# Emitting a convolution and an MLP as one interleaved instruction stream, with work moved between VectorE, ScalarE and GpSimd

## The chip, the cores and the metric

The kernel runs on one core of one Trainium2 chip. The metric is the device time of one execution in microseconds (us), as a median of several executions. The "span" of a profile runs from the first to the last instruction and is some 2 us shorter than the time of the same execution. A run carries a state, fast or slow. All comparisons here use fast runs.

A ratio below is the mean time of one kernel's fast runs over the mean time of the other's fast runs of the same rounds. It is therefore not quite the ratio of the medians that stand beside it. The square brackets after a ratio are its 95% interval.

Names of engines in the profile: PE is TensorE (matmul), PEld its weight load, DVE is VectorE, ACT is ScalarE, POOL is GpSimd, SP is SyncE, which issues DMAs here. A name with a q at its end, such as SPq, is that engine's sequencer.

## The reference, cut to what matters

The input is one sequence of 2048 tokens with 640 channels. Two branches read it, and a gate of one value per token mixes them.

```python
x = A_q                                             # [1, 2048, 640], bf16
g = sigmoid((x * gate_w).sum(-1, keepdims=True))    # gate

# branch A: long convolution
k_shift = sum over t < 4 of shifted(k, 3-t) * shift_k[:, t]   # short filter, "k shift"
kv = k_shift * v
y  = irfft(rfft(kv, 4096) * rfft(ssm_k, 4096))[:2048] + kv * ssm_D
a  = q * y

# branch B: token mixer, then MLP
h  = gelu(layernorm(x) @ w1)                        # 640 -> 640
x1 = x + token_shifted(h) @ w2
b  = x1 + gelu(layernorm(x1) @ w3) @ w4             # 640 -> 1536 -> 640
return g * a + (1 - g) * b
```

## The kernel before

All data stay on the chip. A *slab* is 128 tokens (one per partition), and there are 16 of them. The Fourier transforms are matmuls. The channels are split into two halves `dh` and the frequencies into two halves `h`, so there are four rounds. Each round has an *h pass* (transform of the filter) and an *x pass* (transform of `kv`, product with the filter, first half of the inverse). After the two rounds of a channel half comes `inv`. Between the two stages of a transform, data must change partitions, and that is a DMA from SBUF to SBUF, the *exchange*: `GR` to `gx` in a pass, `VR` to `vx` in the inverse.

```python
def exchange(dst, stage, lo):
    nc.sync.dma_start(out=dst, in_=stage.rearrange("(a r) t d -> a r t d", a=8)[:, lo])

def step1(src, dh, h, isH):                 # first stage: 16 matmuls, 8 ScalarE copies to GR
    ...
def x_pass(dh, h):
    step1(KV, dh, h, False)
    for kp in range(T1 // 2):               # 8 pairs
        ps = pst()
        gx = ring.tile([P, 2, DH], BF16, name="gx", bufs=3)
        for j in range(2):
            exchange(gx[:, j, :], GR, 2 * kp + j)
            nc.tensor.matmul(ps[:, j, 0:DH], lhsT=M3[:, 0, :], rhs=gx[:, j, :], ...)
        xs = ring.tile([P, 2, DH], BF16, name="xs")
        nc.scalar.copy(out=xs[:], in_=ps[:, :, 0:DH])
        pq = ring.tile([P, 2, 2, DH], BF16, name="pq", tag="pv", bufs=3)
        nc.vector.tensor_tensor(out=pq[:], in0=xs[:]..., in1=HH[:, 2 * kp:2 * kp + 2], op=ALU.mult)
        pv = pst()
        for j in range(2):                  # needs pq of this very pair
            nc.tensor.matmul(pv[:, j, 0:DH], lhsT=M3[:, 1, :], rhs=pq[:, j, 0, :], ...)
            nc.tensor.matmul(pv[:, j, 0:DH], lhsT=M3[:, 2, :], rhs=pq[:, j, 1, :], ...)
        nc.scalar.copy(out=VR[:, h, 2 * kp:2 * kp + 2, :], in_=pv[:, :, 0:DH])

def inv(dh):
    for tp in range(T1 // 2):
        ...
            for h in range(2):
                exchange(vx[:, j, h, :], VR[:, h], t1)       # 64 transfers of 80 KB in all
                nc.tensor.matmul(ps[:, j, 0:DH], lhsT=I1[:, h, t1, :], rhs=vx[:, j, h, :], ...)
        nc.vector.tensor_tensor(out=g, in0=ps[:, :, 0:DH], in1=g, op=ALU.mult)
# ... cut: layer norms, W1, W2, gate, k shift ...
w1_chunk(0) ... gate(); mix_shift(); h_pass(0, 0)
for s in range(T1): w2_slab(s)
i1_transposes(); kshift(0) ... kshift(3)
x_pass(0, 0); h_pass(0, 1); w3_chunk(0); x_pass(0, 1); w4_chunk(0)
h_pass(1, 0); gq_half(0); inv(0); w3_chunk(1); x_pass(1, 0); h_pass(1, 1)
w4_chunk(1); w3_chunk(2); x_pass(1, 1); gq_half(1); inv(1)
# ... cut: adds and stores around w4_chunk(2), w3_chunk(3), w4_chunk(3)
```

The traces show the stages on every engine in the order of these calls, with small overlaps only: in the last inverse some w4 matmuls (L461, written later) run between inverse matmuls (L428) from 472.05 us on.

Of the kernel before, what the change touches and what calls it, by code (L numbers as in the profile page):

```python
# [24 lines left out]
def kernel(  # L25
# [55 lines left out]
    R9 = big.tile([P, DT * Fh], BF16, name="R9")  # L81
# [3 lines left out]
    VR = R3.rearrange("p (h t d) -> p h t d", h=2, t=T1)  # L85
    KRG = R3[:, 0:2 * 7 * D].rearrange("p (b t d) -> p b t d", b=2, t=7)
# [6 lines left out]
    ACC = R4[:, 5 * D:7 * D].rearrange("p (t d) -> p t d", t=2)  # L93
    KTMP = R4[:, 7 * D:11 * D].rearrange("p (b t d) -> p b t d", b=2, t=2)
    CJB = GR[:, 0:8, :].rearrange("p k d -> p (k d)")
    MIX = I1[:, 0]
    GEN = HT.rearrange("p t d -> p (t d)")
    NANG = R11[:, 0:8192].bitcast(I32)
    W1 = R9[:, 0:DT * D].rearrange("p (k e) -> p k e", k=DT)
    W2 = R9[:, DT * D:2 * DT * D].rearrange("p (k e) -> p k e", k=DT)  # L100
    W1M = R9[:, 2 * DT * D:2 * DT * D + D].rearrange("p (k e) -> p k e", k=DT)
    W3 = R9.rearrange("p (k f) -> p k f", k=DT)
# [4 lines left out]
    for c in range(4):  # L107
        nc.sync.dma_start(out=QX[:, 4 * c:4 * c + 4, :], in_=q3[:, 4 * c:4 * c + 4, :])
# [10 lines left out]
    def load_k(c):  # L119
        kr = KRG[:, c % 2]  # L120
        if c == 0:
            nc.gpsimd.memset(kr[0:1, 0:3, :], 0.0)
            nc.sync.dma_start(out=kr[1:113, 0:3, :], in_=k3[0:112, 13:16, :])
            nc.sync.dma_start(out=kr[113:128, 0:3, :], in_=k3[112:127, 13:16, :])
            nc.sync.dma_start(out=kr[:, 3:7, :], in_=k3[:, 0:4, :])
        else:
            nc.sync.dma_start(out=kr[:], in_=k3[:, 4 * c - 3:4 * c + 4, :])
        nc.sync.dma_start(out=KV[:, 4 * c:4 * c + 4, :], in_=v3[:, 4 * c:4 * c + 4, :])

    load_k(0)  # L130
    load_k(1)
    for gi in range(4):
        nc.sync.dma_start(out=W2[:, gi, :], in_=B_w2[gi * CG:gi * CG + P, :])
        nc.sync.dma_start(out=W2[32 * gi:32 * gi + 32, 4, :], in_=B_w2[gi * CG + P:(gi + 1) * CG, :])

# [19 lines left out]
    BPI = cons.tile([P, 1], F32, name="BPI")  # L155
    nc.vector.memset(BPI[:], -PI)
    s16 = f32(iot(T1, [[1, T1]], 0, T1), T1)
    wcol = f32(iot(256, [[128, 2], [0, 2], [2, 64]], 1), 256)
    ocol = f32(iot(256, [[0, 2], [-2048, 2], [0, 64]], 6144), 256)
    for g in range(4):  # L160
        n1 = NANG[:, g * 1024:(g + 1) * 1024]
        for j in range(4):
            t1 = 4 * g + j
            nc.vector.scalar_tensor_tensor(out=n1[:, j * 256:(j + 1) * 256], in0=wcol, scalar=s16[:, t1:t1 + 1],
                                           in1=ocol, op0=ALU.mult, op1=ALU.add)
        nc.vector.tensor_scalar(out=n1, in0=n1, scalar1=8191, scalar2=None, op0=ALU.bitwise_and)
        nc.scalar.activation(out=F1[:, 4 * g:4 * g + 4, :, :].rearrange("p a b c -> p (a b c)"), in_=n1,
                             func=ACT.Sin, scale=PI / 4096, bias=BPI[:])

    M3 = cons.tile([P, 3, P], BF16, name="M3")  # L170
    prow = iot(1, [[1, 1]], 0, 1)
    tr = gtile(3, I32)
    for i, bits in enumerate((15, 48, 64)):
        nc.vector.tensor_scalar(out=tr[:, i:i + 1], in0=prow, scalar1=bits, scalar2=None, op0=ALU.bitwise_and)
    trf = f32(tr, 3)
    N3 = 3 * P
    ck1f = f32(iot(N3, [[0, 24], [1, 16]]), N3)
    cof = gtile(N3, I32)
    for m, (stp, b0) in enumerate(((12, 12), (4, 12), (4, 8))):
        nc.gpsimd.iota(cof[:, m * P:(m + 1) * P], pattern=[[stp, 2], [0, 64]], base=b0, channel_multiplier=0)  # L180
    coff = f32(cof, N3)
    crm = gtile(N3, F32)
    for m, val in enumerate((4.0 / 64, 8.0 / 64, 0.0)):
        nc.gpsimd.memset(crm[:, m * P:(m + 1) * P], val)
    cklf = f32(iot(P, [[0, 2], [16, 4], [0, 16]]), P)
    an = gtile(N3, F32)
    nc.vector.scalar_tensor_tensor(out=an, in0=ck1f, scalar=trf[:, 0:1], in1=coff, op0=ALU.mult, op1=ALU.add)
    ani = gtile(N3, I32)
    nc.vector.scalar_tensor_tensor(out=ani, in0=crm, scalar=trf[:, 2:3], in1=an, op0=ALU.mult, op1=ALU.add)
    nc.vector.tensor_scalar(out=ani, in0=ani, scalar1=15, scalar2=None, op0=ALU.bitwise_and)  # L190
    sn = gtile(N3, F32)
    nc.scalar.activation(out=sn, in_=ani, func=ACT.Sin, scale=PI / 8, bias=BPI[:])
    mask = gtile(P, F32)
    nc.vector.tensor_scalar(out=mask, in0=cklf, scalar1=trf[:, 1:2], scalar2=None, op0=ALU.is_equal)
    for m in range(3):
        nc.vector.tensor_tensor(out=M3[:, m, :], in0=sn[:, m * P:(m + 1) * P], in1=mask, op=ALU.mult)
# [4 lines left out]
    ONE1 = cons.tile([1, P], BF16, name="ONE1")  # L201
    nc.gpsimd.memset(ONE1[:], 0.0)
    nc.gpsimd.memset(ONE1[:, 0:64], 1.0)
    NHALF = cons.tile([P, T1], F32, name="NHALF")
    nc.gpsimd.memset(NHALF[:], -0.5)
# [8 lines left out]
    def stats_group(slabs):  # L214
        n = len(slabs)
        st = ring.tile([P, n, 2, 6], F32, name="bst")
        mv = ring.tile([P, n, 2], F32, name="mv")
        for i, s in enumerate(slabs):
            for j in range(2):
                nc.vector.bn_stats(out=st[:, i, j, :], in_=QX[:, s, j * DH:(j + 1) * DH])  # L220
            nc.vector.bn_aggr(out=mv[:, i, :], in_=st[:, i, :, :])
        ve = ring.tile([P, n], F32, name="ve")
        nc.gpsimd.tensor_scalar(out=ve[:], in0=mv[:, :, 1], scalar1=1e-5, scalar2=None, op0=ALU.add)
        rs = ring.tile([P, n], F32, name="rs")
        nc.gpsimd.tensor_tensor(out=rs[:], in0=ve[:], in1=NHALF[:, 0:n], op=ALU.pow)
        nb = ring.tile([P, n], F32, name="nb")
        nc.vector.scalar_tensor_tensor(out=nb[:], in0=mv[:, :, 0], scalar=-1.0, in1=rs[:], op0=ALU.mult, op1=ALU.mult)
        return rs, nb

    def norm_transpose(slabs, rs, nb, dst, eng, after=None):  # L230
        for i0 in range(0, len(slabs), 2):
            pt = pst16()
            for j in range(2):
                s = slabs[i0 + j]
                xn = ring.tile([P, D], BF16, name="xn", tag="xy", bufs=3)
                nc.vector.tensor_scalar(out=xn[:], in0=QX[:, s, :], scalar1=rs[:, i0 + j:i0 + j + 1],  # L236
                                        scalar2=nb[:, i0 + j:i0 + j + 1], op0=ALU.mult, op1=ALU.add)
                if after is not None:
                    after(s)
                for k in range(DT):  # L240
                    nc.tensor.transpose(out=pt[:, j, k * P:(k + 1) * P], in_=xn[:, k * P:(k + 1) * P], identity=IDN[:])  # L241
            o = dst[:, :, i0 * P:(i0 + 2) * P].rearrange("p k (j t) -> p j k t", j=2)
            i_ = pt[:, :, 0:D].rearrange("p j (k t) -> p j k t", k=DT)
            if eng == "act":
                nc.scalar.copy(out=o, in_=i_)  # L245
            else:
                nc.vector.tensor_copy(out=o, in_=i_)  # L247

    def w1_chunk(c):
        slabs = list(range(4 * c, 4 * c + 4))  # L250
        rs, nb = stats_group(slabs)
        xt = XNT[:, c % 2]
        norm_transpose(slabs, rs, nb, xt, "act")
        for n0 in (0, 2, 4):
            ps = pst()
            nn = 1 if n0 == 4 else 2
            for j in range(nn):
                nt = n0 + j
                for k in range(DT):
                    if nt < 4:  # L260
                        lhsT = W1[:, k, nt * CG:nt * CG + P]
                    else:
                        lhsT = W1M[:, k, :]
                    nc.tensor.matmul(ps[:, j, :], lhsT=lhsT, rhs=xt[:, k, :], start=(k == 0), stop=(k == DT - 1))  # L264
            if nn == 2:
                nc.scalar.activation(out=GST[:, n0:n0 + 2, 4 * c:4 * c + 4, 1:129],
                                     in_=ps[:].rearrange("p j (t c) -> p j t c", t=4), func=ACT.Gelu_apprx_tanh)
            else:
                nc.scalar.activation(out=MIX[:, 4 * c:4 * c + 4, :],
                                     in_=ps[:, 0, :].rearrange("p (t c) -> p t c", t=4), func=ACT.Gelu_apprx_tanh)  # L270
# [162 lines left out]
    def rsum(s):  # L433
        nc.vector.tensor_tensor(out=QX[:, s, :], in0=QX[:, s, :], in1=KV[:, s, :], op=ALU.add)
# [117 lines left out]
```

## Time and profile before

| | before |
|---|---|
| time, median of 2 runs | 526.69 us (524.35 to 529.03) |
| span, mean granted clock | 522.9 us, 0.728 |
| busy: PE, DVE, ACT, POOL | 317.2, 216.5, 159.0, 19.7 us |
| first matmul of an x pass, first product `pq`, last product | 137.8, 142.0, 447.9 us |

The first view is the page of the profile of the kernel before: an engine's busy time with its share of the span and its instructions, then the span in 40 slices of 13 us. A digit is the busy share in tenths. PEclk is the TensorE clock that the throttle granted, in tenths of full speed.

```profile
PE 317.2 (61%) x1597; PEld 159.9 (31%) x1608; DVE 216.5 (41%) x444; ACT 159.0 (30%) x214; POOL 19.7 (4%) x49
...
PE   0196654992146459446945488355488835559797
DVE  6988999999841020321201140121014041344402
...
PEclk9998985896555659755965569556579955558899
```

Until the end of the tenth slice (131 us) VectorE is nearly full (92% busy). After that no engine is full for long. PE alternates between 4 and 9, and the clock follows it: 5 or 6 where PE is half idle, 9 where MLP blocks run.

The second view gives stretches of the span: start and end, length, busy time and instructions of each engine, then clock, DMA share and GB/s. The stretches are the end of the VectorE part, the first x pass, an MLP block, part of the first inverse, and the last inverse.

```profile
core 0: us, PE busy (x) PEld busy (x) DVE busy (x) ACT busy (x) POOL busy (x), PEclk, DMA share, GB/s
92.00:113.00 21.00, 21.00 (x143) 14.47 (x143) 19.87 (x28) 0.70 (x1) 0.00 (x0) 0.92 0.26 79
138.00:169.00 31.00, 14.86 (x51) 6.78 (x50) 13.19 (x32) 10.29 (x16) 1.70 (x4) 0.50 0.14 34
194.00:214.00 20.00, 17.22 (x74) 7.68 (x76) 3.42 (x12) 9.64 (x13) 0.00 (x0) 0.91 0.26 63
262.00:282.00 20.00, 7.92 (x23) 1.58 (x21) 0.00 (x0) 9.14 (x15) 0.00 (x0) 0.60 0.42 97
450.00:476.00 26.00, 15.07 (x46) 4.59 (x45) 10.58 (x18) 0.69 (x1) 0.00 (x0) 0.53 0.48 116
```

In the first x pass (138 to 169) every engine is at most half busy. The timeline shows why: start, duration, engine, line, operation, output and input, and in square brackets the idle time before it with what ended it.

```profile
154.33 0.74 PE L399 MATMUL ps<-gx,M_140 128*128 128x320 bf16 x2
...
155.16 0.70 ACT L401 CAST xs<-ps 128x640 bf16<-128x640 f32 x1
155.89 0.83 DVE L403 TENSOR_TENSOR pq<-xs,R_71 128x1280 bf16<-128x1280 bf16 x1 [2.63 <-ACT xs L401]
156.77 0.42 PE L407 MATMUL ps<-pq,M_140 128*128 128x320 bf16 x1 [1.70 <-DVE pq L403]
```

A pair is a chain: two matmuls, a ScalarE copy of 0.70 us, a VectorE product of 0.83, then four matmuls that need the product. The next pair starts 3.46 us after this one (157.79). The list of waits of the kernel before (who waited for whom: total us, times, longest) gives the sums of the waits for the exchange in the h passes (L385) and in the inverses (L428):

```profile
PE ps L407 <- DVE pq L403: 56.8, 32, 4.2
...
PE ps L385 <- DMA gx<-GR: 48.4, 46, 5.3
...
PE ps L428 <- DMA vx<-R_70: 19.4, 35, 3.3
```

The Trainium skill ("TensorE: Matmul & The Clock Gate", Part 1) says that the throttle sets the clock by how busy PE has just been. This trace agrees: 0.50 in the x pass, 0.91 in the MLP block.

### The profile page before, as it was taken

What the parts mean: (1) busy time and instruction counts of PE and PEld (TensorE: products, weight loads), DVE (VectorE), ACT (ScalarE), POOL (GpSimd) and SP (SyncE); (2) the same over time, 40 slices, a digit from 0 to 9 for tenths busy, and PEclk for the clock granted to TensorE, in tenths of its full rate; (3) what the DMA queues carried; (4) which work ended last, traced back from release to release, by engine and by line L of the source; (5) the groups of instructions that cost most, each with busy time, mean ns of one, the idle gap of its engine ahead of it and who ended that gap; (6) DMA issues with size and microseconds to landing.
All of it is one profiled execution on the core that took longest, in us unless ns stands there. A gap on an engine that the chain in (4) does not pass through costs nothing.

```text
span 522.9 us, 4484 instructions
## 1 busy us (share of the span) xinstructions
PE 317.2 (61%) x1597; PEld 159.9 (31%) x1608; DVE 216.5 (41%) x444; ACT 159.0 (30%) x214; POOL 19.7 (4%) x49
## 2 busy tenths in 40 slices
PE   0196654992146459446945488355488835559797
PEld 0163320670022124123611143122055312115455
DVE  6988999999841020321201140121014041344402
ACT  0534553005033423533052016335301633100030
POOL 5121000000200000000000000000000000000000
PEclk9998985896555659755965569556579955558899
DMA  8970206403610250521125510210520241344001
GB/s 326 373 269 0 89 14 140 137 8 146 200 42 8 61 128 13 145 52 38 43 59 127 116 26 0 66 36 2 136 64 0 64 104 36 76 101 150 25 1 50
DMA packets 47638, 45.34 MB, mean 87 GB/s; under 512 B 2688, under 2 KB 44545, under 8 KB 47232
## 3 DMA queue, kind: packets, MB, share of 16 engines
q1 hardware_dynamic: 47616, 45.06, 31.0%
q8 instruction: 12, 0.20, 0.2%
q14 instruction: 10, 0.08, 0.0%
HBM read 21.46 MB, written 2.62 MB: 46 GB/s over the span
## 4 chain that ended last, share of the span: by engine, by line
PE 35%; DVE 26%; DMA 18%; ACT 9%; issue 6%; SPq 3%; POOL 1%; ACTq 0%
DMA gx<-GR 12%; PE ps L451 11%; PE ps L461 10%; DMA vx<-R_70 5%; DVE pq L403 5%; ACT GR L376 4%; PE ps L407 4%; ACT xs L401 4%; DVE bst L220 4%; PE ps L408 3%; SPq L364 3%; DVE R_72 L358 2%; DVE junk L315 2%; DVE R_72 L359 2%; PE ps L302 2%
## 5 line engine op out<-in xcount | busy, mean ns | idle before, releaser
L403 DVE TENSOR_TENSOR pq<-xs,R_71 128x1280 bf16<-128x1280 bf16 x32 | 26.4, 824 | 97.2 <-ACT xs L401 97.2
L407 PE MATMUL ps<-pq,M_140 128*128 128x320 bf16 x64 | 28.7, 449 | 56.8 <-DVE pq L403 56.8
L453 ACT ACTIVATE R_78<-ps 128x1024 bf16<-128x1024 f32 x24 | 24.6, 1024 | 120.8 <-PE ps L451 120.8
L451 PE MATMUL ps<-XNT,R_76 128*128 128x512 bf16 x232 | 56.1, 399 | 5.6 <-DVE XNT L247 4.7
L385 PE MATMUL ps<-gx,M_140 128*128 128x320 bf16 x64 | 27.9, 436 | 49.4 <-DMA gx<-GR 48.4
L461 PE MATMUL ps<-R_72,R_78 128*128 128x320 bf16 x384 | 57.7, 314 | 0.0
L464 DVE SCALAR_TENSOR_TENSOR QX<-ps,OMG,QX 128x640 bf16<-128x640 f32 x16 | 14.1, 884 | 81.3 <-PE ps L461 81.3
L376 ACT CAST GR<-ps 128x640 bf16<-128x640 f32 x64 | 39.1, 733 | 20.7 <-PE ps L373 20.7
L461 PEld LDWEIGHTS <-R_78 128*128 128x128 bf16 x384 | 39.3, 102 | 18.6 <-issue 1.0
L409 ACT CAST R_70<-ps 128x640 bf16<-128x640 f32 x32 | 22.1, 692 | 72.1 <-PE ps L408 72.1
L399 PE MATMUL ps<-gx,M_140 128*128 128x320 bf16 x64 | 24.2, 468 | 22.4 <-DMA gx<-GR 22.3
L386 ACT ACTIVATE R_71<-ps 128x640 bf16<-128x640 f32 x32 | 22.5, 704 | 49.4 <-PE ps L385 49.4
L428 PE MATMUL ps<-vx,I_75 128*128 128x320 bf16 x64 | 25.3, 440 | 19.9 <-DMA vx<-R_70 19.4
L451 PEld LDWEIGHTS <-R_76 128*128 128x128 bf16 x240 | 24.5, 103 | 36.2 <-issue 10.1
L431 DVE TENSOR_TENSOR KV<-ps,KV 128x640 bf16<-128x640 f32 x16 | 13.2, 825 | 52.5 <-PE ps L428 52.5
L241 PE MATMUL pt<-IDN,xn 128*128 128x128 bf16 x160 | 15.1, 254 | 29.4 <-DVE xn L236 29.2
L408 PE MATMUL ps<-pq,M_140 128*128 128x320 bf16 x64 | 30.2, 472 | 0.0
L408 PEld LDWEIGHTS <-M_140 128*128 128x128 bf16 x64 | 8.1, 127 | 70.8 <-issue 67.1
L220 DVE BATCH_NORM_STATS2 bst<-QX 128x6 f32<-128x320 bf16 x64 | 27.7, 468 | 4.3 <-DMA QX<-in_A_q_dram 4.3
L264 PE MATMUL ps<-XNT,R_76 128*128 128x512 bf16 x97 | 25.3, 417 | 5.9 <-ACT XNT L245 5.6
L401 ACT CAST xs<-ps 128x640 bf16<-128x640 f32 x32 | 22.3, 696 | 19.5 <-PE ps L399 19.5
L385 PEld LDWEIGHTS <-M_140 128*128 128x128 bf16 x64 | 4.2, 110 | 71.1 <-DMA gx<-GR 71.1
(79 smaller groups left out, 348.9 us busy)
## 6 DMA issues: line engine op xcount, KB each, us to landing
gx<-GR SPq DMA_DIRECT2D x128, 80.0 KB
R_71<-R_71 SPq DMA_DIRECT2D x16, 320.0 KB
vx<-R_70 SPq DMA_DIRECT2D x64, 80.0 KB
R_70<-in_A_k_dram SPq DMA_DIRECT2D x3, 1120.0 KB
QX<-in_A_q_dram SPq DMA_DIRECT2D x4, 640.0 KB
R_71<-in_A_ssm_k_dram SPq DMA_DIRECT2D x5, 512.0 KB
KV<-in_A_v_dram SPq DMA_DIRECT2D x4, 640.0 KB
KV<-in_A_q_dram SPq DMA_DIRECT2D x8, 320.0 KB
```

The costliest lines, as they stand in the source:

```text
L220: nc.vector.bn_stats(out=st[:, i, j, :], in_=QX[:, s, j * DH:(j + 1) * DH])
L264: nc.tensor.matmul(ps[:, j, :], lhsT=lhsT, rhs=xt[:, k, :], start=(k == 0), stop=(k == DT - 1))
L376: nc.scalar.copy(out=GR[:, 2 * tp:2 * tp + 2, :], in_=ps[:, :, 0:DH])
L385: nc.tensor.matmul(ps[:, j, 0:DH], lhsT=M3[:, 0, :], rhs=gx[:, j, :], start=True, stop=True)
L401: nc.scalar.copy(out=xs[:], in_=ps[:, :, 0:DH])
L403: nc.vector.tensor_tensor(out=pq[:], in0=xs[:].unsqueeze(2).to_broadcast([P, 2, 2, DH]), in1=HH[:, 2 * kp:2 * kp + 2], op=ALU.mult)
L407: nc.tensor.matmul(pv[:, j, 0:DH], lhsT=M3[:, 1, :], rhs=pq[:, j, 0, :], start=True, stop=False)
L408: nc.tensor.matmul(pv[:, j, 0:DH], lhsT=M3[:, 2, :], rhs=pq[:, j, 1, :], start=False, stop=True)
L428: nc.tensor.matmul(ps[:, j, 0:DH], lhsT=I1[:, h, t1, :], rhs=vx[:, j, h, :], start=(h == 0), stop=(h == 1))
L451: nc.tensor.matmul(ps[:, j, :], lhsT=W3[:, k, (f0 + j) * P:(f0 + j + 1) * P], rhs=xt[:, k, :], start=(k == 0), stop=(k == DT - 1))
L453: nc.scalar.activation(out=GTP[:, (3 * c + f0 // 4) % 5, f0 % 4:f0 % 4 + 2, :], in_=ps[:], func=ACT.Gelu_apprx_tanh)
L461: nc.tensor.matmul(ps[:, j, 0:DH], lhsT=GTP[:, (3 * c + f // 4) % 5, f % 4, i * P:(i + 1) * P], rhs=W4[:, f, j * DH:(j + 1) * DH], start=( ...
```

## The change

Intent: give PE MLP matmuls to do while it would wait for the convolution, keep the clock up by that, and take work off VectorE before 131 us. The diff has over 800 lines. Its core, with cuts marked:

```diff
+    def x_step2(h, lag):                     # x pass, pipelined by one pair; a generator
+        pqs = {}
+        for i in range(T1 // 2 + 1):
+            if i < T1 // 2:
+                ... exchange, two matmuls, ScalarE copy xs, VectorE product pq of pair i ...
+            if i >= 1:
+                pq = pqs.pop(i - 1)          # four matmuls of the pair before
+                ...
+            yield (0.84 if i else 0.28), (lag if i == T1 // 2 else 1.0)
...
+    def conv():                              # step1, h_step2, x_step2, inv in one generator
+    def mlp2():                              # w3 half groups, w4 thirds of a slab: pieces of about 1.1 us
+    def mix(a, b, ta, tb, each=None):        # emits the next piece of whichever is behind by weight;
+        ...                                  # a convolution step may ask for a lag before its successor
+            if la and (not lb or (clock >= na and da / ta <= db / tb)):
+                r = next(a, None)
...
+    mix(cv, m2, 57.4, 86.0)
+    for s in range(12, 16):                  # what is left: four w4 slabs, adds and stores
+        addy(s)
+        for _ in w4_slab(s):
+            pass
+        store(s)
...
     def w2_slab(s):                          # residual add gives the norm's sum; ScalarE the squares
-        nc.vector.tensor_tensor(out=x, in0=ps[:, :, 0:DH], in1=x, op=ALU.add)
+        nc.vector.scalar_tensor_tensor(out=x, in0=ps[:, :, 0:DH], scalar=1.0, in1=x, ..., accum_out=SUM[:, s:s + 1])
+        nc.scalar.activation(out=JK, in_=QX[:, s, :], func=ACT.Square, accum_out=SQS[:, s:s + 1])
...
     # gate: product on VectorE, its sum on ScalarE
-            nc.vector.scalar_tensor_tensor(out=junk[:], in0=QX[:, s, :], scalar=1.0, in1=GW[:], ..., accum_out=Z[:, s:s + 1])
+        nc.vector.tensor_tensor(out=pr[:], in0=QX[:, s, :], in1=GW[:], op=ALU.mult)
+        nc.scalar.activation(out=JK, in_=pr[:], func=ACT.Identity, accum_out=Z[:, s:s + 1])
...
     # angles of the Fourier table F1
-            nc.vector.scalar_tensor_tensor(out=n1[:, j * 256:(j + 1) * 256], in0=wcol, scalar=s16[:, t1:t1 + 1],
-                                           in1=ocol, op0=ALU.mult, op1=ALU.add)
+                    nc.gpsimd.tensor_scalar(out=n1v[:, j, :, c, :], in0=wv[:, :, c, :], scalar1=s16[:, t1:t1 + 1],
+                                            scalar2=6144.0 - 2048.0 * c, op0=ALU.mult, op1=ALU.add)
...
     # inverse: one transfer of 160 KB for both h, in place of two of 80 KB
-                    exchange(vx[:, j, h, :], VR[:, h], t1)
+                nc.sync.dma_start(out=vx[:, j], in_=VR.rearrange("(a r) t h d -> a r t (h d)", a=8)[:, t1])
...
     # gate times q: four loads and 16 VectorE products per half become one load; the gate goes into the last add
-                nc.vector.tensor_scalar(out=KV[:, s, ds], in0=KV[:, s, ds], scalar1=G32[:, s:s + 1], ...)
+        nc.vector.scalar_tensor_tensor(out=QX[:, s, :], in0=KV[:, s, :], scalar=G32[:, s:s + 1], in1=QX[:, s, :], ...)
```

The k shift became a generator too. It is "pumped" a few operations at a time between W2 slabs and MLP pieces. The first norm works on pairs of slabs, and loads were reordered. `mlp2` has only w4 slabs 0 to 11, and slabs 12 to 15 follow after the last inverse.

## The prediction

> **What bounds it now.** No engine: busy shares are PE 61%, DVE 41%, ACT 30% of 522.9 us (engine page). The chain of waits shows two regimes.
>
> 1. 0 to about 131 us is VectorE: busy 94-100% in the windows 61-73 and 92-127 us. It does layer-norm statistics, the gate (16 x 0.82 us), the k shift (64 operations of 0.82 us, spaced 0.74) and the residual adds.
> 2. 131 to 523 us is latency, stages one after another: four convolution x passes of 31-33 us, three h passes of 20-25, two inverses of 24 and 26, and the MLP pieces (w3 chunks of 13-14 us, w4 chunks of 14.5-15). In an x pass a pair takes 3.46 us in the timeline: matmul, ScalarE copy 0.70, VectorE product 0.82, four matmuls; PE waits 2.6 of it. In h passes and inverses PE waits for exchange DMAs (gx 48 us, vx 19 us in the list of waits; 0.72-0.87 us apart). The granted clock is 0.50-0.57 there, 0.86-1.00 in the MLP windows. The Trainium skill (TensorE: Matmul & The Clock Gate, Part 1) says the throttle is the idle default and activity releases it; this trace agrees.
>
> **What the change does.**
> - It interleaves convolution steps with w3/w4 half groups, pipelines the x pass by one pair, and leaves 4 lag units after step 1 for the exchange. Matmul work is the same, about 1.1 us per piece at full clock (12.9-13.9 us per 12 w3 half groups).
> - VectorE: second-norm statistics go (16 x 1.07 = 17 us), gate multiplies fall from 0.90 to about 0.45 (7 us), table angles move to POOL (6.8 us). Accumulator reads and halo splits add about 4 us.
> - ScalarE gets 32 accumulating passes, estimate 0.7 us each (as its 128x640 copies): 22 us, where it has room. POOL gets 32 small multiplies and longer statistics chains.
> - 64 vx transfers become 32 of double size.
>
> **Costed in three parts (estimates from these durations).**
> - To the start of the interleaved part (first x pair): VectorE work before 131 falls by a net 10-14 us to about 117, plus first-load wait 5 and gaps: 125 us. Four w3 groups are by then also done.
> - Interleaved part: walking the change's own order and weights, 130 of its 145 weighted us have both kinds of work. Stalls on top: ScalarE drains step-1 bursts at 0.61 us per copy against 0.28 of PE (4 x 2.6), h steps want 1.45-1.75 us for two exchanges against 1.38 allowed (8), four PSUM buffers shared (10), w4 at 0.15 us per matmul (4), sundry (10): 172 us.
> - Tail: the MLP runs out before the convolution. Alone remain half an h pass 7, step 1 and first exchange 8, the last x pass pipelined 8 x 1.8 + 3, the last inverse 17, w4 slabs 12-15 with stores 17: 67 us, at low clock.
>
> Sum 364; I add 8 for what in-order engines lose: **372 us, range 342 to 410.** Chances: faster 0.97, within 2% 0.02, slower 0.01. Of about 150 us gained, nearly all is the MLP's 112 us of PE time hidden under the convolution plus the x pipelining (4 x 12 us).
>
> **Right if:** granted clock in the middle is above 0.85 and PE busy above 80%; an x pair without MLP beside it takes about 1.8 us, not 3.46; GR copies in bursts are 0.61 apart; second-norm statistics are gone; the last 60-70 us show low clock and DMA waits.
>
> **Wrong if:** the scheduler reorders the pieces; POOL angles (over 0.6 us each) hold VectorE in the first 30 us; PSUM or ScalarE stalls make a half group plus x step cost far over 2 us (over 410 us); or w4 slabs fill the tail (under 342).

## The result, and the profile after

| | before | after |
|---|---|---|
| time, median of 2 runs | 526.69 us | 375.56 us (374.62 to 376.49) |
| ratio | | 0.713 [0.6974, 0.7287] |
| span, mean granted clock | 522.9 us, 0.728 | 372.8 us, 0.895 |
| busy PE | 317.2 us | 266.4 us |
| first x matmul, first and last product `pq` | 137.8, 142.0, 447.9 us | 127.4, 132.0, 323.2 us |

The time fell by 151 us. The number of matmuls is the same but for a few records (1597 and 1594), yet PE was busy 51 us less: the same matmuls took less time at the higher clock. The page after, with slices of 9.3 us:

```profile
PE 266.4 (71%) x1594; PEld 151.8 (41%) x1608; DVE 186.1 (50%) x339; ACT 184.3 (49%) x280; POOL 57.0 (15%) x139
...
PE   0003999784697979998499998679998635634594
DVE  5326999999799985120254113231630002323286
...
PEclk9999999989699989999789999899999865655589
DMA  7997400322046254047830446531402656144424
```

From the 15th to the 31st slice (131 to 289 us) PE and the clock are mostly at 8 or 9. In most of the last nine slices PE falls back to 3 to 6 and the clock to 5 or 6: this is the part of the convolution with no MLP work left to stand beside it. Only the last w4 slabs, at the very end, bring both up again. In the first slices VectorE has less to do than before (5, 3, 2), and the reason is not that it is free, as the start below shows. The stretches after are: the VectorE part, the interleaved part, the end of the last h pass with step 1, the last x pass, the last inverse, and the rest.

```profile
35.00:131.00 96.00, 80.75 (x558) 49.04 (x564) 92.01 (x185) 69.11 (x118) 31.02 (x66) 0.95 0.28 72
131.00:290.00 159.00, 137.14 (x817) 79.05 (x824) 49.16 (x71) 86.91 (x126) 1.02 (x2) 0.96 0.40 96
290.00:304.70 14.70, 6.85 (x26) 2.44 (x24) 0.00 (x0) 9.12 (x14) 0.00 (x0) 0.78 0.63 138
304.70:325.60 20.90, 13.28 (x48) 6.14 (x48) 6.60 (x8) 10.40 (x16) 0.00 (x0) 0.58 0.44 119
325.60:354.00 28.40, 11.73 (x35) 3.69 (x36) 8.24 (x10) 0.00 (x0) 0.00 (x0) 0.50 0.47 110
354.00:372.80 18.80, 13.98 (x95) 9.46 (x92) 14.51 (x18) 0.00 (x0) 0.00 (x0) 0.94 0.32 114
```

In the interleaved part PE is busy 137.14 of 159 us (86%) at a clock of 0.96. From 290 us on there are 83 us, and of these only the last 19 run at a high clock.

The timeline of one x pair in the interleaved part:

```profile
269.80 0.43 PE L429 MATMUL ps<-gx,M_103 128*128 128x320 bf16 x2
...
270.07 0.30 PE L440 MATMUL ps<-pq,M_103 128*128 128x320 bf16 x1
...
270.27 0.69 ACT L431 CAST xs<-ps 128x640 bf16<-128x640 f32 x1 [0.61 <-PE ps L429]
...
270.62 1.25 PE L509 MATMUL ps<-R_72,R_78 128*128 128x320 bf16 x8
...
271.00 0.83 DVE L433 TENSOR_TENSOR pq<-xs,R_71 128x1280 bf16<-128x1280 bf16 x1 [1.07 <-ACT xs L431]
...
271.70 0.43 PE L429 MATMUL ps<-gx,M_103 128*128 128x320 bf16 x2
```

This is the same chain as before, yet PE does not wait. L440 works on the product of the pair before, and while ScalarE copies and VectorE multiplies, PE runs eight w4 matmuls (L509). A pair with its piece of MLP takes 1.9 us, against 3.46 for the pair alone before. In the list of waits after, the first, the third and the fourth line answer to the three shown of before; the second is new:

```profile
PE ps L458 <- DMA vx<-R_70: 23.4, 23, 4.1
...
DVE R_78 L172 <- POOL R_78 L170: 12.3, 4, 3.4
...
PE ps L414 <- DMA gx<-GR: 8.4, 18, 1.1
...
PE ps L440 <- DVE pq L433: 4.0, 5, 1.3
```

The wait for the product fell from 56.8 to 4.0 us, the h passes' wait for the exchange from 48.4 to 8.4. The wait for the inverse's exchange did not fall: 19.4 us before, 23.4 after. And VectorE now waits 12.3 us for GpSimd. The start of the timeline after shows that wait:

```profile
10.19 16.41 POOL L170 TENSOR_SCALAR R_78<-HT 128x128 int32<-128x128 f32 x32 [1.56 <-DVE HT L149]
14.19 0.69 DVE L172 TENSOR_SCALAR R_78<-R_78 128x1024 int32<-128x1024 int32 x1 [2.96 <-POOL R_78 L170]
...
18.47 0.69 DVE L172 TENSOR_SCALAR R_78<-R_78 128x1024 int32<-128x1024 int32 x1 [2.95 <-POOL R_78 L170]
```

GpSimd takes 16.41 us for the 32 angle operations, and VectorE stands in order behind each quarter of them. Its norms, which W1 needs, are queued behind. And the end of the timeline after:

```profile
306.38 0.60 SPq L447 DMA_DIRECT2D KV<-in_A_q_dram  x1
...
314.05 0.45 PE L429 MATMUL ps<-gx,M_103 128*128 128x320 bf16 x1 [3.42 <-DMA gx<-GR]
...
330.55 0.69 PE L458 MATMUL ps<-vx,I_75 128*128 128x320 bf16 x2 [0.87 <-DMA vx<-R_70]
...
332.16 0.71 PE L458 MATMUL ps<-vx,I_75 128*128 128x320 bf16 x2 [0.92 <-DMA vx<-R_70]
```

In the last inverse two matmuls take 0.7 us and PE then waits 0.9 us for the next transfer: one transfer of 160 KB lands about every 1.6 us. Before that, in the last x pass, one exchange lies behind the load of the second half of q (KV from A_q, 1280 KB, issued at 306.38).

### The profile page after: what moved, and what is told of

The parts are those of the page before. It is cut to its first block, busy times and chain, and to the rows that moved or that the text cites. A ratio compares the mean times of both kernels' runs of the same rounds, so it can differ in the third digit from the quotient of the medians.

```text
span 372.8 us, 4494 instructions
## 1 busy us (share of the span) xinstructions
PE 266.4 (71%) x1594; PEld 151.8 (41%) x1608; DVE 186.1 (50%) x339; ACT 184.3 (49%) x280; POOL 57.0 (15%) x139
## 4 chain that ended last, share of the span: by engine, by line
DVE 25%; PE 23%; DMA 22%; ACT 8%; POOL 7%; issue 7%; SPq 7%; DVEq 0%; ACTq 0%
DMA gx<-GR 14%; DMA vx<-R_70 6%; PE ps L509 6%; DVE R_72 L372 6%; ACT GR L400 5%; PE ps L496 5%; SPq L456 5%; POOL R_78 L170 4%; DVE R_72 L375 3%; PE ps L440 2%; DVE QX L318 2%; DVE QX L485 2%; SPq L387 2%; PE ps L441 2%; DVE pq L433 2%
## 5 line engine op out<-in xcount | busy, mean ns | idle before, releaser
L496 PE MATMUL ps<-XNT,R_76 128*128 128x512 bf16 x230 | 62.6, 393 | 1.1 <-ACT GR L400 0.3
L509 PE MATMUL ps<-R_72,R_78 128*128 128x320 bf16 x384 | 59.0, 304 | 0.3 <-ACT GR L400 0.2
L509 PEld LDWEIGHTS <-R_78 128*128 128x128 bf16 x384 | 38.2, 99 | 18.6 <-issue 3.3
L458 PE MATMUL ps<-vx,I_75 128*128 128x320 bf16 x64 | 18.3, 387 | 23.5 <-DMA vx<-R_70 23.4
L496 PEld LDWEIGHTS <-R_76 128*128 128x128 bf16 x240 | 24.0, 101 | 25.9 <-issue 6.4
L260 PEld LDWEIGHTS <-xn 128*128 128x128 bf16 x160 | 12.3, 112 | 43.4 <-DVE xn L257 40.0
L429 PE MATMUL ps<-gx,M_103 128*128 128x320 bf16 x64 | 18.0, 349 | 15.5 <-DMA gx<-GR 15.3
L315 PE MATMUL ps<-R_76,R_78 128*128 128x320 bf16 x160 | 26.7, 323 | 2.3 <-issue 2.1
L257 DVE TENSOR_SCALAR xn<-QX,rs,mb 128x640 bf16<-128x640 bf16 x32 | 13.5, 438 | 26.5 <-PE pt L260 21.1
L277 PE MATMUL ps<-XNT,R_76 128*128 128x512 bf16 x96 | 24.7, 402 | 2.3 <-ACT XNT L265 2.1
L440 PE MATMUL ps<-pq,M_103 128*128 128x320 bf16 x64 | 20.6, 332 | 4.5 <-DVE pq L433 4.0
L414 PE MATMUL ps<-gx,M_103 128*128 128x320 bf16 x64 | 17.2, 304 | 8.9 <-DMA gx<-GR 8.4
L372 DVE TENSOR_TENSOR R_72<-R_70,R_72 128x1280 bf16<-128x1280 bf16 (+3 forms) x32 | 23.2, 750 | 0.0
```

Source lines behind the costliest of these rows:

```text
L260: nc.tensor.transpose(out=pt[:, j, k * P:(k + 1) * P], in_=xn[:, k * P:(k + 1) * P], identity=IDN[:])
L277: nc.tensor.matmul(ps[:, j, :], lhsT=lhsT, rhs=xt[:, k, :], start=(k == 0), stop=(k == DT - 1))
L315: nc.tensor.matmul(ps[:, j, 0:DH], lhsT=gst_ap(k, s), rhs=W2[:, k, j * DH:(j + 1) * DH], start=(k == 0), stop=(k == DT - 1))
L372: nc.vector.tensor_tensor(out=dst[:, a:b], in0=src, in1=cj, op=ALU.mult)
L496: nc.tensor.matmul(ps[:, j, :], lhsT=W3[:, k, (f0 + j) * P:(f0 + j + 1) * P], rhs=xt[:, k, :], start=(k == 0), stop=(k == DT - 1))
L509: nc.tensor.matmul(ps[:, j, 0:DH], lhsT=GTP[:, (3 * c + f // 4) % 5, f % 4, i * P:(i + 1) * P], rhs=W4[:, f, j * DH:(j + 1) * DH], start=( ...
```

## The experiments

**The theory** (the prediction's): the engines work in order, so that time is lost where PE stands behind a chain or a DMA. Interleaving puts MLP matmuls into these gaps, pipelining shortens the chain, and what is left over is the part where the MLP has run out. **The rival:** the other edits (pipelining, less VectorE work, fewer transfers) make most of the gain and the interleaving adds little, or other engines take it back. There are smaller questions on every term. Twelve kernels ran, on three chips. The kernel before ran beside them each time, with medians of 526.65, 527.65 and 527.11 us. The changed kernel itself was not run again beside them, so its 375.6 us (two runs) is compared by way of the kernel before. Differences of 3 us or less to it are weak for that reason. Its own ratio has a wide interval (0.6974 to 0.7287), with which those of runs 4, 5, 8, 9 and 10 overlap; of these five, only run 9 has times within the 374.62 to 376.49 us of the changed kernel. For them the shifts in the traces must carry the argument. All results agreed with the reference.

### 1. Interleaving undone, all else kept

```diff
-    mix(cv, m2, 57.4, 86.0)
+    for na_, nb_ in ((9, 0), (16, 17), (17, 17), (24, 16), (33, 16), (0, 16), (25, 0)):
+        for _ in range(na_): next(cv, None)      # whole passes of the convolution
+        for _ in range(nb_): next(m2, None)      # whole blocks of the MLP
+    for _ in cv: pass
+    for _ in m2: pass
```

> The changed kernel, but from the first x pair on whole convolution passes alternate with blocks of 16-17 MLP pieces, as the kernel before had them; all else of the change stays. Theory A (the gain is MLP matmul time hidden under the latency of the convolution): the 82 pieces left, about 1.1 us each, come back on the time: 450 to 475 us. Rival B (x pipelining, fewer VectorE passes and fewer transfers made the gain; interleaving adds little because the waits are elsewhere): 385 to 415 us.

Measured: 441.86 us (440.96 to 444.63, 4 runs), ratio 0.8392 [0.8355, 0.8429], clock 0.814. This is 66 us over the changed kernel. It is nearer to the first expectation than to the second, but below its range. The chain that ended last (start, us, what) has the MLP blocks in it, alone, as four groups; some of their long pieces:

```profile
173.51 6.47 PE ps L496 x30
179.98 7.61 PE ps L509 x56
...
273.97 13.04 PE ps L509 x96
...
345.38 13.04 PE ps L509 x96
```

The four groups run from 171.0 to 187.6, 213.4 to 229.0, 270.7 to 289.2 and 332.7 to 367.1 us, which makes 85 us. From the first product to the last inverse matmul this kernel takes 290.5 us (130.6 to 421.1), and the changed kernel 221.6 us (132.0 to 353.6). So 205 us of convolution without company became 222 us of convolution with the MLP inside. Interleaving hides 85 us of MLP and lengthens the convolution by some 16; net about 69, of which the time shows 66. So the rival is wrong in that the interleaving adds little. It is right in that the other edits together make the larger part: 151 less 66 are 85 us. What the higher clock (0.895 against 0.814) is worth by itself, apart from the filled gaps, no run separates.

### 2. Pipelining of the x pass undone in the changed kernel

```diff
-        for i in range(T1 // 2 + 1):       # product of pair i, matmuls of pair i-1
+        for i in range(T1 // 2):           # product and matmuls of pair i
...
-            yield (0.84 if i else 0.28), (lag if i == T1 // 2 else 1.0)
+            yield 0.84, (lag if i == T1 // 2 - 1 else 1.0)
```

> The changed kernel with the x pass not pipelined: the four matmuls of a pair follow the same pair's product at once. If pieces of the MLP between the steps cover the wait just as well, only the last x pass (alone) loses 8 x 1.3 us: 383 to 388 us. If, as I hold, PE takes its instructions in order and so waits about 1.7 us for copy and product inside every one of the 32 pairs, the cost is 40 to 55 us: 415 to 430 us.

Measured: 426.02 us (423.86 to 429.12), ratio 0.8087 [0.8047, 0.8127], 50 us over the changed kernel. The wait of PE for the product is back:

```profile
PE ps L435 <- DVE pq L431: 44.1, 28, 4.4
```

The MLP pieces emitted between steps do not fill this gap, because it lies inside a step. PE starts nothing else meanwhile: in this run's timeline it stands 1.96 us before the product's matmul at 209.47, and the w3 matmuls follow only at 210.01. To gain fully, interleaving needs steps that don't wait inside themselves.

### 3. The kernel before with the x pass pipelined, nothing else

The edit gives `x_pass` of the kernel before the loop of `x_step2`, without any MLP.

> The kernel before with nothing but the x pass pipelined by one pair. Theory A: a pair falls from 3.46 us to the 1.75-1.8 us that its two exchange transfers take, 32 pairs: about 45 to 52 us less, 475 to 482 us. Rival B (pipelining makes the larger part of the gain): under 450 us.

Measured: 470.14 us (468.83 to 471.57), ratio 0.8921 [0.8884, 0.8957]. That is 56.5 us less than before, 5 us below the expected range: the products of a pass start 1.65 us apart on the average instead of 3.46, and 32 pairs times 1.81 make 58. With run 1 this splits the 151 us in this order of edits: pipelining 56.5, all other edits but interleaving 28 (470.1 to 441.9), interleaving 66.

### 4. Table angles back on VectorE, in the changed kernel

```diff
-                    nc.gpsimd.tensor_scalar(out=n1v[:, j, :, c, :], in0=wv[:, :, c, :], scalar1=s16[:, t1:t1 + 1],
-                                            scalar2=6144.0 - 2048.0 * c, op0=ALU.mult, op1=ALU.add)
+                nc.vector.scalar_tensor_tensor(out=n1[:, j * 256:(j + 1) * 256], in0=wcol, scalar=s16[:, t1:t1 + 1],
+                                               in1=ocol, op0=ALU.mult, op1=ALU.add)
```

> The changed kernel with the table angles back on VectorE (16 operations of about 0.48 us) in place of 32 on POOL. If VectorE's 12.3 us of waiting for POOL in the first 30 us is on the critical path, the start comes 8-9 us earlier and VectorE has 7 us more work, some of it in time it waited: 366 to 372 us. If VectorE's load up to 130 us alone counts: 378 to 383 us.

Measured: 367.46 us (364.99 to 369.21, 6 runs), ratio 0.6973 [0.6939, 0.7008]: 8 us faster than the changed kernel. The first W1 matmuls, after and in this run (durations least/median/most in ns, first and last start):

```profile
L277 PE MATMUL ps<-XNT,R_76 x96: 377/379/634, 35.1 to 67.6; 128*128 128x512 bf16 x96
```

```profile
L276 PE MATMUL ps<-XNT,R x96: 377/379/635, 26.1 to 58.9; 128*128 128x512 bf16 x96
```

They start 9.0 us earlier, and the first product 6.7 us earlier (125.3). Besides VectorE, GpSimd's own share of the norms stood behind the angles too (its operation for the second pair of slabs starts at 27.89 us after, at 9.81 in this run), and VectorE waited 5.3 us for such operations in the changed kernel; no run separates the two. This part of the change worked against it. The Trainium skill ("GPSIMD Engine Reference", section 4.1 Engine selection) tells to give elementwise work to VectorE, and the traces agree for this case: GpSimd needs 16.4 us for 32 operations of 128 columns (0.51 apart), VectorE before needed 1.66 us for four of 256 columns. GpSimd was idle, but VectorE had to stand behind it.

### 5 and 6. The sums of the second norm, and of the gate, back on VectorE

```diff
 # run 5
-        nc.vector.scalar_tensor_tensor(out=x, ..., accum_out=SUM[:, s:s + 1])
-        nc.scalar.activation(out=JK, in_=QX[:, s, :], func=ACT.Square, accum_out=SQS[:, s:s + 1])
+        nc.vector.tensor_tensor(out=x, in0=ps[:, :, 0:DH], in1=x, op=ALU.add)
-            stats2(s // 2)
+            stats1(s // 2)                  # the statistics instruction of VectorE
 # run 6: run 5, and
-        nc.vector.tensor_tensor(out=pr[:], in0=QX[:, s, :], in1=GW[:], op=ALU.mult)
-        nc.scalar.activation(out=JK, in_=pr[:], func=ACT.Identity, accum_out=Z[:, s:s + 1])
+        nc.vector.scalar_tensor_tensor(out=pr[:], in0=QX[:, s, :], scalar=1.0, in1=GW[:], ..., accum_out=Z[:, s:s + 1])
```

> The changed kernel with the second norm's statistics again from VectorE's own statistics instruction (32 of about 0.46 us spaced 0.42, 16 of 0.2), the residual add without its sum, no squares on ScalarE. Theory: VectorE is full from 35 to 131 us, so about 16 us of its work comes back there, less 1.3 for the accumulator reads: 386 to 392 us. Rival: in that stretch the POOL and ScalarE chain or the h pass's exchange bounds the adds, and the sums bought nothing: 373 to 379 us.

> As the run before it, and the gate's sum is back on VectorE too (16 operations of 0.82 + 0.08 us in place of 0.49). Against e5: theory 16 x 0.45 = 6-7 us more on VectorE, less the ScalarE passes that the exchange waited for at 73-83 us: 390 to 398 us in all. If ScalarE's accumulating passes (0.74 + 0.19 us each) were themselves on the way between 71 and 90 us, it is no slower than e5.

Measured: 385.44 us (384.39 to 386.75, 5 runs), ratio 0.731 [0.7281, 0.7339], and 389.99 us (389.68 to 394.05, 6 runs), ratio 0.7405 [0.7372, 0.7437]. Run 5 is 9.9 us over the changed kernel, and run 6 is 4.5 us over run 5; both lie just below their expected ranges. The first product moves from 132.0 to 138.3 to 142.6 us. VectorE bounds the part before the first x pass (busy 92 of the 96 us from 35 to 131 in the changed kernel). Its busy time grows by 13.3 and 5.3 us in the two runs; of these 18.6 us the time shows 14.4, and 10.6 of them lie before the first product. ScalarE pays for it with 32 more passes of 0.74 us.

### 7. Large pieces in place of small ones

```diff
-            if j == 0:
-                yield 1.1, 0.0              # half of a w3 group
...
-        yield 1.1, 0.0
+        yield 2.2, 0.0                      # a whole w3 group
...
-            if f in (3, 7):
-                yield 1.1, 0.0              # a third of a w4 slab
...
-        yield 1.1, 0.0
+        yield 3.3, 0.0                      # a whole w4 slab
...
-    for _ in range(8):                      # the pieces before the mixing: half as many, twice as large
+    for _ in range(4):
         next(m2)
-        pump(5)
+        pump(10)
```

> The changed kernel with the MLP handed out in whole groups: 20 wide matmuls of two rows at once are still one w3 group of 2.2 us, a whole w4 slab is 3.3 us. If the smallness of the pieces matters, each coarse piece makes the convolution's step wait about 1.1-2.2 us longer in some 36 of its steps: 390 to 410 us. If only the total counts: 372 to 380 us.

Measured: 401.74 us (401.09 to 403.19), ratio 0.762 [0.7581, 0.7659]. First product 132.0 us as in the changed kernel, last product 350.9 against 323.2, clock 0.88 from 131 to 316. The time lies in the first expected range. So the small pieces are worth 26 us of the 66. The reason is argued, not shown: a convolution step that is ready in the middle of a slab waits for the rest of it, by the weights up to 3.3 us.

### 8 and 9. The inverse's exchange: two transfers of 80 KB, and two issuing queues

```diff
 # run 8
-                nc.sync.dma_start(out=vx[:, j], in_=VR.rearrange("(a r) t h d -> a r t (h d)", a=8)[:, t1])
                 for h in range(2):
+                    nc.sync.dma_start(out=vx[:, j, h], in_=VR[:, :, h].rearrange("(a r) t d -> a r t d", a=8)[:, t1])
 # run 9
-                nc.sync.dma_start(out=vx[:, j], in_=...)
+                (nc.scalar if j else nc.sync).dma_start(out=vx[:, j], in_=...)
```

> The changed kernel with the inverse's inputs again in 64 transfers of 80 KB instead of 32 of 160 KB. After the run with two queues I hold that these transfers move about 100 GB/s however they are cut: 374 to 379 us, last inverse 26-27 us. If merging them was worth what I had predicted (17 us for an inverse against 24-26 before), it is 385 us or more.

> The changed kernel with every second vx transfer of the inverse started from ScalarE's queue, so two queues share the exchange. My inverse alone took 27 us where I had put 17. If one queue's issue (1.35 us for 160 KB) is the limit, both inverses halve their transfer time: 360 to 368 us, the last inverse 15-18 us. If the transfers themselves are the limit at about 100 GB/s: 373 to 379 us and the last inverse stays near 26 us.

Run 9: 377.46 us (375.81 to 379.68), ratio 0.7157 [0.7122, 0.7193]. The second queue helps nothing, and the last inverse takes 25 us from its first matmul (330.4 to 355.3), as in the changed kernel (329.0 to 354). The Trainium skill ("DMA: Bandwidth & Descriptors", section "Issuing engines are not separate DMA queues") says that transfers from several issuing engines share the same 16 DMA engines. This run agrees: not the issue but the transfer is the limit.

Run 8 missed its expectation. Three fast runs took 368.09, 369.22 and 369.70 us, ratio 0.6998 [0.696, 0.7036], that is about 6 us less than the changed kernel. To merge the transfers did not gain, and seems to have cost. Why is not shown, but the traces hold a likely part of it. Before, the first four transfers of the last inverse were issued from 443.10 us on, ahead of the last copy to `VR` (450.02), and its first matmuls ran at 449.78. After the merging the first transfer is issued at 325.58, behind the last copy (324.87), and PE then waits 4.13 us for it; a merged transfer needs both halves `h`. How much of the 6 us this makes, no trace of a fast run tells, because the only profile of run 8's kernel fell into the slow one of its four runs, which took 1408.64 us. That run is left out of all comparisons. Its page, and its inverse matmuls:

```profile
PE 1361.8 (97%) x1608; PEld 499.8 (36%) x1608; DVE 190.2 (14%) x339; ACT 195.0 (14%) x280; POOL 59.5 (4%) x139
```

```profile
L458 PE MATMUL ps<-vx,I x64: 770/1185/1362, 957.9 to 1329.3; 128*128 128x320 bf16 x64
```

Other engines show their usual busy times, but a matmul of 320 columns took 1.185 us (median), in place of 0.30 to 0.47, and the record of the clock says 1.000 for the whole run. The result was correct. No experiment explains this run.

### 10. The second half of q loaded early

```diff
-        nc.sync.dma_start(out=KV[:, :, ds], in_=q3[:, :, ds])
+        nc.sync.dma_start(out=(HT if dh else KV)[:, :, ds], in_=q3[:, :, ds])   # HT is free by then
... (the product with q reads HT in the second half)
                     yield from step1(HT, dh, h, True, LAG)
+                    if (dh, h) == (1, 1):
+                        q_half(1)
...
-        q_half(1)                           # before the last inverse
```

> The changed kernel with the second half of q (1280 KB) loaded earlier, into the filter's tile, which is free after its last step 1, and no longer in the midst of the last x pass. There PE waited 3.4 us for an exchange transfer just after that load was started (310.6 to 314.1 us). If the load held up the exchange: 370 to 373 us, and the last x pass shows no such wait. If the load only moves the wait into the h pass it now lies in: 374 to 378 us.

Measured: 372.41 us (370.96 to 373.53), ratio 0.7061 [0.7026, 0.7097]: 3.2 us less than the changed kernel, in the expected range. The wait of 3.42 us in the last x pass is gone from the trace, and the products of that pass span 11.0 us instead of 16.5. But they begin 4.8 us later (311.5 against 306.7), and the h pass beside which the load now lies waits 2.48 us for an exchange (at 290.38). So the delay was in part moved, as the second expectation said; that what is left is the size of the one wait is chance. The intervals of the two ratios overlap.

### 11. The tail: w4 slabs 12 to 15 into the interleaving, adds and stores after each inverse step

```diff
+        for s in range(12, 16):
+            yield from w4_slab(s)           # at the end of mlp2
...
-        yield from inv(1)
+        for tp, r in enumerate(inv(1)):
+            for s in (2 * tp, 2 * tp + 1):
+                addy(s)
+                store(s)
+            yield r
...
-    mix(cv, m2, 57.4, 86.0)
-    ... the loop over slabs 12 to 15 ...
+    mix(cv, m2, 57.4, 99.2)
```

> The changed kernel with w4 slabs 12-15 inside the interleaved part as well, and the adds and stores of each pair of rows right after its step of the last inverse. The 19 us after the last inverse shrink to 4-5 us if nothing else takes their place: 359 to 364 us. If the stores (2.6 MB) slow the inverse's transfers as the theory of a shared transfer rate says, part of it comes back: 364 to 371 us.

Measured: 364.39 us (363.99 to 367.93), ratio 0.6926 [0.6885, 0.6966], 11.2 us less than the changed kernel. The 14 us of w4 matmuls after the last inverse are gone, but the inverse itself takes 26 us from its first matmul (330.3 to 356.4) at a clock of 0.50 with 154 GB/s of DMA, stores included:

```profile
328.00:362.00 34.00, 11.24 (x32) 3.08 (x32) 19.32 (x24) 0.00 (x0) 0.00 (x0) 0.50 0.57 154
```

The time lies where the two expected ranges meet, so it does not decide whether the stores slow the transfers. The last inverse waits for its transfers, and moving the rest did not change that.

### 12. Runs 4, 10 and 11 together

The edits are the three above, in one kernel.

> The angles on VectorE, the early load of q and the tail inside the inverse, together on the changed kernel. If the three gains add (8, 3 and 8-15 us): 350 to 358 us, and faster than both kernels by over 4%. If they overlap: 358 to 365 us.

Measured: 357.88 us (357.32 to 358.48, 5 runs), ratio 0.679 [0.6759, 0.682]. This is 17.7 us (4.7%) less than the changed kernel and faster than both kernels. The single gains were 8.1, 3.2 and 11.2 us, which makes 22.5, so they don't quite add up. First product 125.0 us, last 317.9, last inverse matmul 349.0, clock 0.908.

## Why the prediction was right or wrong

The prediction was 372 us (342 to 410), and 375.56 us came. Its sum of three parts was 364 plus 8 for what in-order engines lose. The parts measured in the trace after:

| part | predicted | measured | |
|---|---|---|---|
| start to first x pair | 125 | 127.4 | first x matmul at 127.4 us |
| interleaved part | 172 | 163 | 127.4 to the end of the MLP's w3 at about 290 |
| tail | 67 | 83 | 290 to 372.8 |
| of which half an h pass and step 1 | 15 | 15 | 290 to 304.7 |
| of which last x pass | 17.4 | 21 | 304.7 to 325.6 |
| of which last inverse | 17 | 28 | 325.6 to 354; 25 from its first matmul |
| of which w4 slabs and stores | 17 | 19 | 354 to 372.8 |

- **The total: in part luck.** The start came 2.4 us late, the middle 9.4 early and the tail 15.8 late, and the 8 us of reserve took up the difference.
- **What bounds it: right.** Runs 2 and 3 show the chain inside the pair (50 and 56 us), run 1 shows the stages that stood one after another (66 us).
- **The middle: right.** PE busy 86% (above 80%), clock 0.96 (above 0.85). The stalls were put 9 us too high. One reading was wrong without consequence: "PE waits 2.6 of it" is VectorE's wait for the copy (2.63 us); PE waits 1.70.
- **The start: right in sum only.** The prediction lists 17 + 7 + 6.8 us less for VectorE and 4 more, some 27 in all, and then takes off only 10 to 14. The sums moved to ScalarE (17 + 7) were worth 14.4 us (runs 5 and 6). The angles moved to GpSimd, counted as a gain of 6.8 us, cost 8 us instead (run 4). The prediction named this danger but put its threshold at "over 0.6 us each"; the operations came 0.51 us apart, and that already held VectorE for 12.3 us. What counted was not the cost of one but the 16 us of the whole row in front of the norms. That the sum fitted all the same is luck: the items were too large, and the deduction was smaller than their sum.
- **The tail: the step that failed.** "The last inverse 17" measured 28 us. The profile before showed the last inverse at 26 us (450 to 476), with PE waiting for the exchange. Nothing in the change makes that transfer faster: in the last inverse 80 KB landed every 0.86 us before, which is 95 GB/s, and 160 KB every 1.69 us after, 97 GB/s (medians of the intervals between landings in the traces). Halving the number of transfers saved nothing here, where each has twice the bytes. And 3 to 4 of the 28 us are the wait for the first merged transfer. The prediction's "last 60-70 us show low clock" fails at the end too: the w4 slabs run at 0.94. Run 9 shows that the issuing queue is not the limit, and in run 11 the inverse still took 26 us although w4 work was gone from behind it and adds and stores ran beside it.
- **The last x pass: right in kind.** Pairs alone came 1.6 to 2.3 us apart (predicted 1.8), with one wait of 3.42 us for an exchange behind the load of q, which was not foreseen (run 10).
- **Where the 150 us come from: half right.** "The MLP's 112 us of PE time hidden" is mis-sized: only 85 us of it stood alone to be hidden, and the convolution grew by 16 while hiding it (run 1), so the term is worth 66 to 69. "x pipelining (4 x 12)" was 48 predicted and 50 to 56 measured. Of the remaining 28 us, in order of edits, 15 lie before the first product (145.7 us in run 3, 130.6 in run 1), where the VectorE work named above was; where the other 13 lie no run shows.

Why does a transfer between partitions run at only about 100 GB/s? The Trainium skill ("DMA: Bandwidth & Descriptors", section "Why a DMA increments its semaphore by 16 and not by 1") says that the number of DMA engines used is the largest number up to 16 that divides the outermost sizes of both access patterns. The source pattern of the exchange has 8 as its outermost size, which gives an estimate of 8 of 16 engines; the DMA share of the last inverse, 0.48 before and 0.47 after, fits it. The packets in the trace of the changed kernel, counted one by one, bear it out: from 328 to 352 us exactly 8 packets are under way at once for 14.8 of the 24 us, while it is 16 most often during the first loads (6 to 12 us). They show a second cause: a packet of 1280 bytes takes 94 ns (median) in this exchange, but 56 ns in the stores at the end, and 8 times 1280 bytes in 94 ns make 109 GB/s. The copies inside the filter's tile (`R_71` to `R_71`, 320 KB, also from SBUF to SBUF) have 16 packets under way most often, and pairs of them land 1.4 to 1.7 us apart: about 190 to 230 GB/s. So a pattern with 16 outermost would be the next thing to try; no run tests it. Open are why the packets of the exchange are slow, the 6 us of run 8, and its slow run.

## What to carry to other kernels

Interleaving two streams pays what stood alone to be hidden, less what the other stream grows by, and it pays fully only after each piece has been freed of waits inside itself and cut small: without pipelining the changed kernel lost 50 us, with pieces two or three times as large 26 us. Moving work to an idle engine gains where the busy one no longer waits for it (sums at the end of a chain, 14 us), and loses where the busy one stands in order behind it (angles at its start, 8 us). For a stage that waits for transfers, read its length from the trace, and don't let it shrink in the estimate unless the change touches the bytes per second; then see what is left standing alone at the end, because the next gain lies there.

## What the Trainium skill lacked or had wrong

- "DMA: Bandwidth & Descriptors", section "Anatomy of one DMA — SWDGE (gpsimd) path": a fixed part of about 2 us and the bytes at 436 GB/s, for transfers that GpSimd issues. For SBUF to SBUF the page has a ceiling of the fabric, but no measured figure for transfers that change partitions. Here such transfers, issued by SyncE, landed every 0.86 us per 80 KB and every 1.69 us per 160 KB, that is 95 to 97 GB/s, with half of the DMA engines' time busy.
- "GPSIMD Engine Reference", section 4.1: it calls GpSimd roughly line-rate for one-input operations. Here a one-input multiply-add of 128 columns from float to integer took 372 ns (median) and came every 0.51 us, whereas VectorE did 256 columns with two inputs in 478 ns, one every 0.41 us: about 2.5 times as fast per column (0.51/128 against 0.41/256). How much of GpSimd's time is a fixed part of each small operation, no run separates. The page says nothing of the order in which a waiting VectorE stands behind it, which here cost 8 us.
- "TensorE: Matmul & The Clock Gate", Part 1, warns that the clock's records can be unreliable and that a low clock can last over 50 us. Run 8 goes much further: one execution of 1408.64 us in which matmuls of 320 columns took 1.185 us all through the inverses, with a recorded clock of 1.000.
- "ScalarE: Activation LUTs" mentions an accumulator output but no cost for reading it. Here each was a second instruction of 188 ns beside a pass of 735 ns, 32 times.
